# Loading and storing the first four rows of a layer-scale kernel by halves over two DMA rings

## The chip, the cores and the metric

The kernel runs on one core of one Trainium2 chip. The metric is device time in microseconds (us), as the median of several runs. Before the change it is 119.79 us (6 runs, 119.58 to 119.87).

## The reference

```python
x, y: bf16 [1024, 16, 512]      gamma: bf16 [512]
def reference(x, y, gamma):
    return x + gamma * y
```

Flattened, x, y and the output have 16,384 rows of 512 values, 1 KB each. So 16.8 MB of x and as much of y are read, and 16.8 MB are written.

## The kernel before

Each of the 128 partitions of the on-chip memory holds 128 rows of y (`y_sb`); the result is formed in place and stored from there. x has a smaller buffer (`x_sb`), parts of which are used twice. In what follows a "row" is one of these 128 places per partition, 0 to 127.

The rows are cut into three blocks (`BLOCKS`, L7) of 4, 64 and 60 rows. `rows_of` (L65) maps a block to a contiguous stretch of memory, in which partition p has the p-th share. For the first block, rows 0 to 3, this is 512 KB of memory, and partition p has 4096 B at 4096 p.

All loads and stores are issued from two engines, each with its own DMA ring. Their order is written out by hand:

- `SP` (L12): y 0:4, y 4:68, x 4:68, y 68:128, x 68:120, x 120:128.
- `ACT` (L20): x 0:4, gamma, and the stores of rows 4:68, 0:4 and 68:128.

The function `ring` (L113) issues such a list. Some issues are moved to the very start of the program, ahead of its start barrier (`EARLY`, L22: two of SP's, one of ACT's; L197 to L203). Before the issue with the number in `AHEAD` (L24: SP's third, ACT's second), a ring waits until TensorE has seen the load named `HOLD` land, which is y 0:4 (L147 to L149). VectorE gets the same signal. TensorE then waits for gamma, spreads it over the partitions with one matmul (L152), and VectorE copies it to `gamma_sb` (L154). A second signal from TensorE, when x 68:120 has landed (`RELEASE`, L157 to L159), lets ACT's stores begin.

VectorE works in five pieces (`PIECES`, L9) of 8, 16, 44, 52 and 8 rows. The list `DVE` (L28) is its order: multiply pieces 0, 1, 2; add pieces 2, 0, 1; multiply 3, 4; add 3, 4. Multiplications are L180, additions L189. Each waits for the loads that its piece meets (`need`, L163). x 68:120 and x 120:128 go to places of `x_sb` that earlier rows of x had, so their issue waits for additions (`frees`, L102; L126). A store waits for the additions of its rows. The program ends when all stores have reported on `s_out` (L195).

Of the kernel before, what the change touches and what calls it, by code (L numbers as in the profile page):

```python
# [8 lines left out]
PIECES = [8, 16, 44, 52, 8]  # L9


SP = [  # L12
    ('y', 0, 4),
    ('y', 4, 68),
    ('x', 4, 68, 4),
    ('y', 68, 128),
    ('x', 68, 120, 24),
    ('x', 120, 128, 0),
]
ACT = [('x', 0, 4, 0), ('g',), ('s', 4, 68), ('s', 0, 4), ('s', 68, 128)]  # L20

EARLY = (2, 1)  # L22

HOLD, AHEAD = ('y', 0, 4), (2, 1)  # L24

RELEASE = ('x', 68, 120, 24)

# [4 lines left out]
def _take(sem, n, eng):  # L32


    return eng.wait_ge(sem, n).then_inc(sem, -n)  # L35


def kernel(
    tc: tile.TileContext,
    x: bass.AP,  # L40
    y: bass.AP,
    gamma: bass.AP,
    out: bass.AP,
):

    nc = tc.nc
    P = nc.NUM_PARTITIONS
    tc.close()  # L50
    tc.compile()  # L51

    xf = x.flatten_outer_dims()
    yf = y.flatten_outer_dims()
    of = out.flatten_outer_dims()
    N, D = xf.shape
    rows = N // P
    n = len(PIECES)
    assert sum(PIECES) == rows
    starts = [sum(PIECES[:c]) for c in range(n + 1)]  # L60
    dt = xf.dtype
    edges = [sum(BLOCKS[:c]) for c in range(len(BLOCKS) + 1)]
    assert edges[-1] == rows

    def rows_of(t, a, b):  # L65

        c = max(c for c in range(len(BLOCKS)) if edges[c] <= a)
        assert b <= edges[c + 1]
        block = t[P * edges[c] : P * edges[c + 1]].rearrange("(p n) d -> p n d", p=P)
        return block[:, a - edges[c] : b - edges[c], :]  # L70

    gamma_row = nc.alloc_sbuf_tensor("gamma_row", [1, D], dt).ap()
    ones_row = nc.alloc_sbuf_tensor("ones_row", [1, P], dt).ap()
    gamma_sb = nc.alloc_sbuf_tensor("gamma_sb", [P, D], dt).ap()
    y_sb = nc.alloc_sbuf_tensor("y_sb", [P, rows, D], dt).ap()
    x_loads = [w for w in ACT + SP if w[0] == "x"]
    y_loads = [w for w in SP + ACT if w[0] == "y"]
    stores = [w for w in SP + ACT if w[0] == "s"]
    for loads in (x_loads, y_loads, stores):
        assert sum(w[2] - w[1] for w in loads) == rows  # L80
    x_rows = max(w[3] + w[2] - w[1] for w in x_loads)
    x_sb = nc.alloc_sbuf_tensor("x_sb", [P, x_rows, D], dt).ap()
    gamma_ps = nc.alloc_psum_tensor("gamma_ps", [P, D], mybir.dt.float32).ap()

    sem = nc.alloc_semaphore
    s_gamma, s_ones, s_ps, s_dve = sem("s_gamma"), sem("s_ones"), sem("s_ps"), sem("s_dve")
    s_load = {w: sem("s_" + "_".join(map(str, w[:2]))) for w in x_loads + y_loads}
    s_held = {nc.sync: sem("s_held_sp"), nc.scalar: sem("s_held_act"), nc.vector: sem("s_held_dve")}
    s_add, s_go, s_rel, s_end, s_out = sem("s_add"), sem("s_go"), sem("s_rel"), sem("s_end"), sem("s_out")
    added = [a for kind, *a in DVE if kind == "a"]  # L90
    order = {a[0]: k for k, a in enumerate(added)}

    def meets(a, b, c, d):
        return a < d and c < b

    def pieces_of(a, b):
        return [c for c in range(n) if meets(starts[c], starts[c + 1], a, b)]

    def x_at(row):
        return next(w[3] + row - w[1] for w in x_loads if w[1] <= row < w[2])  # L100

    def frees(w):  # L102

        c = set()
        for v in x_loads[: x_loads.index(w)]:
            lo, hi = max(v[3], w[3]), min(v[3] + v[2] - v[1], w[3] + w[2] - w[1])
            if lo < hi:
                c |= set(pieces_of(v[1] + lo - v[3], v[1] + hi - v[3]))
        return sorted(c)

    early = []

    def ring(eng, what, n_early, n_ahead):  # L113

        known, went = 0, False
        for k, w in enumerate(what):
            kind = w[0]
            if k == n_ahead:
                _take(s_held[eng], 1, eng)
            need = frees(w) if kind == "x" else pieces_of(w[1], w[2]) + list(w[3:]) if kind == "s" else []  # L120
            need = max((order[c] + 1 for c in need), default=0)
            if kind == "s" and not went:
                _take(s_go, 1, eng)
                went = True
            if need > known:
                eng.wait_ge(s_add, need)  # L126
                known = need
            if kind == "g":
                i = eng.dma_start(out=gamma_row, in_=gamma.unsqueeze(0)).then_inc(s_gamma, 16)
            elif kind == "x":  # L130
                to = x_sb[:, w[3] : w[3] + w[2] - w[1], :]
                i = eng.dma_start(out=to, in_=rows_of(xf, w[1], w[2])).then_inc(s_load[w], 16)
            elif kind == "y":
                r = slice(w[1], w[2])
                i = eng.dma_start(out=y_sb[:, r, :], in_=rows_of(yf, w[1], w[2])).then_inc(s_load[w], 16)
            else:
                r = slice(w[1], w[2])
                i = eng.dma_start(out=rows_of(of, w[1], w[2]), in_=y_sb[:, r, :]).then_inc(s_out, 16)
            if k < n_early:
                early.append(i.ins)  # L140

    ring(nc.sync, SP, EARLY[0], AHEAD[0])
    ring(nc.scalar, ACT, EARLY[1], AHEAD[1])


    nc.vector.memset(ones_row, 1.0).then_inc(s_ones, 1)  # L146
    _take(s_load[HOLD], 16, nc.tensor)  # L147
    for s_one in s_held.values():
        nc.tensor.sem_inc(s_one, 1)  # L149
    _take(s_ones, 1, nc.tensor)  # L150
    _take(s_gamma, 16, nc.tensor)
    nc.tensor.matmul(gamma_ps, ones_row, gamma_row, start=True, stop=True).then_inc(s_ps, 1)  # L152
    _take(s_ps, 1, nc.vector)
    nc.vector.tensor_copy(out=gamma_sb, in_=gamma_ps).then_inc(s_dve, 1)  # L154
    _take(s_dve, 1, nc.vector)

    _take(s_load[RELEASE], 16, nc.tensor)  # L157
    nc.tensor.sem_inc(s_go, 1)
    nc.tensor.sem_inc(s_rel, 1)  # L159

    landed, open_mults = set(), 0

    def need(loads, c):  # L163
        for w in loads:
            if w not in landed and meets(starts[c], starts[c + 1], w[1], w[2]):
                if w == RELEASE:
                    _take(s_rel, 1, nc.vector)
                elif w == HOLD:
                    _take(s_held[nc.vector], 1, nc.vector)
                else:  # L170
                    _take(s_load[w], 16, nc.vector)
                landed.add(w)

    for kind, *args in DVE:
        c = args[0]
        yt = y_sb[:, starts[c] : starts[c + 1], :]
        if kind == "m":
            need(y_loads, c)
            g = gamma_sb[:, None, :].to_broadcast([P, PIECES[c], D])
            nc.vector.tensor_tensor(out=yt, in0=yt, in1=g, op=MULT).then_inc(s_dve, 1)  # L180
            open_mults += 1
        else:
            need(x_loads, c)
            if open_mults:
                _take(s_dve, open_mults, nc.vector)
                open_mults = 0
            at = x_at(starts[c])
            xt = x_sb[:, at : at + PIECES[c], :]
            nc.vector.tensor_tensor(out=yt, in0=xt, in1=yt, op=ADD).then_inc(s_add, 1)  # L189


    nc.scalar.sem_inc(s_end, 1)
    _take(s_end, 1, nc.sync)
    _take(s_add, n, nc.sync)
    _take(s_out, 16 * len(stores), nc.sync)  # L195

    main = nc.main_func.blocks[0].instructions  # L197
    names = {i.name for i in early}
    for b in nc.main_func.blocks[1:]:
        for i in [i for i in b.instructions if i.name in names]:  # L200
            b.instructions.remove(i)
    for k, i in enumerate(early):
        main.insert(1 + k, i)  # L203
# [30 lines left out]
```

## Time and profile before

| | |
|---|---|
| Median of 6 runs | 119.79 us (119.58 to 119.87) |
| The profiled execution's own time | 119.92 us |
| Its span, first to last instruction | 118.6 us |
| Moved by DMA | 50.33 MB, 424 GB/s on the mean |
| VectorE busy | 70.1 us (59%) |
| Queue q1 (SP's ring) | 864 packets, 33.03 MB |
| Queue q10 (ACT's ring) | 578 packets, 17.30 MB |

The profile is one execution, seen instruction by instruction. The busy line gives each engine's share of the span. The line of digits named DMA cuts the span into 40 equal slices and gives the mean busy share of the core's 16 DMA engines in tenths. The queue lines give packets, megabytes and the share of 16 engines' time that their packets took. In a table of windows, the columns are the window, its length, the busy time of PE, PEld, DVE (VectorE) and POOL, the granted clock, the DMA share and GB/s; the bytes of a packet are counted in the window where it starts. In a timeline a line has start, duration, engine and line of the code; SPq and ACTq are the sequencers that issue DMAs, and their durations are those of the issue, not of the transfer. The list of DMA issues ends in the time from issue to landing.

### The profile page before, as it was taken

The numbers are of one execution on the slowest core, as the hardware profiler recorded it, in microseconds if no ns is written. First come the engines' busy times: TensorE is split into PE (matmuls) and PEld (weight loads), VectorE is DVE, ScalarE is ACT, GpSimd is POOL, SyncE is SP. The second block draws the span as 40 slices with busy tenths as digits, with TensorE's granted clock in tenths as the row PEclk, the third lists the DMA queues.
The fourth block names the chain that finished last, engine by engine and source line by source line (L and its number), as shares of the span: only waits on it lengthen the run. The fifth ranks groups of instructions, "written<-read, shape, count | busy, mean of one in ns | idle before, by whom it ended". The sixth has DMA issues, their size and how long they took to land. (4 is left out here: it accounts for less than half of the span.)

```text
span 118.6 us, 91 instructions
## 1 busy us (share of the span) xinstructions
PE 0.6 (0%) x1; PEld 0.1 (0%) x1; DVE 70.1 (59%) x12; POOL 0.2 (0%) x4
## 2 busy tenths in 40 slices
PE   0000100000000000000000000000000000000000
PEld 0000000000000000000000000000000000000000
DVE  0000200089999969999999999999999900000000
POOL 0000000000000000000000000000000000000000
DMA  6999888998899879977969797798899889799787
GB/s 202 506 398 663 354 354 354 641 420 354 354 553 508 354 332 518 477 332 332 663 287 557 305 557 305 337 658 354 354 508 553 354 354 508 332 580 414 332 352 311
DMA packets 1442, 50.33 MB, mean 424 GB/s; under 512 B 161, under 2 KB 162, under 8 KB 546
## 3 DMA queue, kind: packets, MB, share of 16 engines
q1 hardware_dynamic: 864, 33.03, 65.0%
q10 hardware_dynamic: 578, 17.30, 33.8%
HBM read 33.56 MB, written 16.78 MB: 424 GB/s over the span
## 5 line engine op out<-in xcount | busy, mean ns | idle before, releaser
L180 DVE TENSOR_TENSOR y_sb<-y_sb,gamma_sb 128x4096 bf16<-128x4096 bf16 (+3 forms) x5 | 34.6, 6979 | 11.1 <-DVEq L35 11.1
L189 DVE TENSOR_TENSOR y_sb<-x_sb,y_sb 128x4096 bf16<-128x4096 bf16 (+3 forms) x5 | 34.7, 6981 | 1.2 <-DVEq L35 1.0
L154 DVE CAST gamma_sb<-gamma_ps 128x512 bf16<-128x512 f32 x1 | 0.7, 692 | 10.4 <-DVEq L35 10.4
L146 DVE MEMSET ones_row<- 1x128 bf16 x1 | 0.2, 165 | 2.0 <-PEq L51 2.0
L152 PE MATMUL gamma_ps<-gamma_row,ones_row 1*128 1x512 bf16 x1 | 0.6, 578 | 11.8 <-PEq L35 11.8
L152 PEld LDWEIGHTS gamma_ps<-gamma_row,ones_row 1*128 1x128 bf16 x1 | 0.1, 100 | 11.8 <-issue 11.8
L218 POOL MEMSET const-bfloat16-1.0<- 128x1 bf16 x1 | 0.1, 102 | 0.0
L218 POOL MEMSET const-uint8-127<- 128x1 uint8 x1 | 0.1, 102 | 0.0
L218 POOL MEMSET const-float32-1.0<- 128x1 f32 x1 | 0.1, 99 | 0.0
L218 POOL MEMSET const-float32-0.0<- 128x1 f32 x1 | 0.1, 98 | 0.2 <-issue 0.2
## 6 DMA issues: line engine op xcount, KB each, us to landing
y_sb<-in_y_dram SPq DMA_DIRECT2D x1, 7680.0 KB, 57.3
out_dram<-y_sb ACTq DMA_DIRECT2D x1, 7680.0 KB, 23.8
x_sb<-in_x_dram SPq DMA_DIRECT2D x1, 6656.0 KB, 21.7
x_sb<-in_x_dram SPq DMA_DIRECT2D x1, 1024.0 KB, 22.0
y_sb<-in_y_dram SPq DMA_DIRECT2D x1, 512.0 KB, 3.7
x_sb<-in_x_dram ACTq DMA_DIRECT2D x1, 512.0 KB, 4.7
out_dram<-y_sb ACTq DMA_DIRECT2D x1, 512.0 KB, 22.3
y_sb<-in_y_dram SPq DMA_DIRECT2D x1, 23.7
```

The source lines that it names most:

```text
L146: nc.vector.memset(ones_row, 1.0).then_inc(s_ones, 1)
L152: nc.tensor.matmul(gamma_ps, ones_row, gamma_row, start=True, stop=True).then_inc(s_ps, 1)
L154: nc.vector.tensor_copy(out=gamma_sb, in_=gamma_ps).then_inc(s_dve, 1)
L180: nc.vector.tensor_tensor(out=yt, in0=yt, in1=g, op=MULT).then_inc(s_dve, 1)
L189: nc.vector.tensor_tensor(out=yt, in0=xt, in1=yt, op=ADD).then_inc(s_add, 1)
L218: nc = _bacc.Bacc("TRN2", target_bir_lowering=False, num_devices=1)
```

## The change

The loads of rows 0:4 of y and of x, and the store of these rows, become two DMAs each. Half 0 has the even partitions, half 1 the odd ones. Of the block's 512 KB of memory, half 0 has the first 256 KB and half 1 the second, so that each half is a stretch without gaps; partition 2k + h has the k-th 4096 B of half h. x, y and the output are cut alike. SP issues half 0 of y and of x ahead of y 4:68, ACT half 1 of y and of x ahead of gamma. ACT issues both halves of the store, one after the other, in the place of the one before. All the loads by halves and y 4:68 are issued early; the hold is now on both halves of y, which share one semaphore that TensorE waits on for 32.

```diff
 SP = [
-    ('y', 0, 4),
+    ('y', 0, 4, 'half', 0),
+    ('x', 0, 4, 0, 'half', 0),
     ('y', 4, 68),
     ('x', 4, 68, 4),
     ('y', 68, 128),
     ('x', 68, 120, 24),
     ('x', 120, 128, 0),
 ]
-ACT = [('x', 0, 4, 0), ('g',), ('s', 4, 68), ('s', 0, 4), ('s', 68, 128)]
-
-EARLY = (2, 1)
-
-HOLD, AHEAD = ('y', 0, 4), (2, 1)
+ACT = [
+    ('y', 0, 4, 'half', 1),
+    ('x', 0, 4, 0, 'half', 1),
+    ('g',),
+    ('s', 4, 68),
+    ('s', 0, 4, 'half', 0),
+    ('s', 0, 4, 'half', 1),
+    ('s', 68, 128),
+]
+
+EARLY = (3, 2)
+
+HOLD, AHEAD = [('y', 0, 4, 'half', h) for h in range(2)], (3, 2)
...
-        block = t[P * edges[c] : P * edges[c + 1]].rearrange("(p n) d -> p n d", p=P)
-        return block[:, a - edges[c] : b - edges[c], :]
+        part = t[P * edges[c] : P * edges[c + 1]]
+        if w[-2] == "half":
+            half = P // 2 * (edges[c + 1] - edges[c])
+            part = part[half * w[-1] : half * (w[-1] + 1)].rearrange("(p n) d -> p n d", p=P // 2)
+        else:
+            part = part.rearrange("(p n) d -> p n d", p=P)
+        return part[:, a - edges[c] : b - edges[c], :]
+
+    def at(sb, w, first):
+
+        parts = slice(w[-1], P, 2) if w[-2] == "half" else slice(0, P)
+        return sb[parts, first : first + w[2] - w[1], :]
...
-    s_load = {w: sem("s_" + "_".join(map(str, w[:2]))) for w in x_loads + y_loads}
+    s_load = {w: sem("s_" + "_".join(map(str, w[:2] + w[4:]))) for w in x_loads + y_loads if w not in HOLD}
+    s_hold = sem("s_hold")
+    s_load |= {w: s_hold for w in HOLD}
...
-    _take(s_load[HOLD], 16, nc.tensor)
+    _take(s_hold, 16 * len(HOLD), nc.tensor)
...
-                elif w == HOLD:
-                    _take(s_held[nc.vector], 1, nc.vector)
+                elif w in HOLD:
+                    if w == HOLD[0]:
+                        _take(s_held[nc.vector], 1, nc.vector)
```

## The prediction

> **What bounds the kernel now.** I read the page first: busy time, the 40 slices and the queues.
>
> ```profile
> span 118.6 us, 91 instructions
> PE 0.6 (0%) x1; PEld 0.1 (0%) x1; DVE 70.1 (59%) x12; POOL 0.2 (0%) x4
> DMA  6999888998899879977969797798899889799787
> ...
> DMA packets 1442, 50.33 MB, mean 424 GB/s; under 512 B 161, under 2 KB 162, under 8 KB 546
> ...
> q1 hardware_dynamic: 864, 33.03, 65.0%
> q10 hardware_dynamic: 578, 17.30, 33.8%
> ```
>
> No compute engine is near full: VectorE has 59%. The two DMA queues take 65.0 + 33.8 = 98.8% of the time of 16 DMA engines. Only the first slice (6) shows a real gap. So the time is a head before the first packet, 50.33 MB through 16 engines, and a tail. The chain of waits agrees in its own way: it holds only 10.6% issue and 3.2% VectorE of the span, because what happens inside DMA queues isn't in it.
>
> Next I read the DMA packet records of the trace (queue, start, duration, size). A 65,536 B packet takes 2418 ns, 27.1 GB/s for one engine; a 4096 B packet takes 159 ns, 25.8 GB/s; a completion record takes 9 ns and costs about 15 ns with the step to it. An engine starts its next packet as the last one ends, from about 1.0 to 1.4 us to 117.9 to 118.2 us. That is the proof that each nanosecond added to an engine's packets is added to the end. Reckoned per engine: busy 117.16 us, which with a mean start of 1.16 us makes 118.3 us.
>
> The head is the place of the change, so I cut it into stretches of 0.5 us (the last two columns are the DMA share and GB/s):
>
> ```profile
> 1.00:1.50 0.50, 0.00 (x0) 0.00 (x0) 0.00 (x0) 0.00 (x0) 1.00 1.06 156
> 1.50:2.00 0.50, 0.00 (x0) 0.00 (x0) 0.01 (x1) 0.00 (x0) 1.00 0.90 303
> 2.00:2.50 0.50, 0.00 (x0) 0.00 (x0) 0.16 (x1) 0.00 (x0) 1.00 1.04 393
> 2.50:3.00 0.50, 0.00 (x0) 0.00 (x0) 0.00 (x0) 0.00 (x0) 1.00 0.90 360
> 3.00:3.50 0.50, 0.00 (x0) 0.00 (x0) 0.00 (x0) 0.00 (x0) 1.00 1.04 418
> ```
>
> Bytes are booked where a packet starts, so only stretches of small packets read well. Sixteen engines with 4096 B in 159 ns make 412 GB/s. Against that the five rows lose 0.31 + 0.13 + 0.02 + 0.06 + 0 = about 0.5 us. More than 0.5 us can't be won in the head without an earlier first packet. In the records the first packet of an engine takes 501 ns on the mean (269 to 838), 0.34 us over 159 ns: most of that half microsecond. ACT's ring shows its first packet only at 2.57 us, after six or seven packets of SP's on each engine, although ACT issued at 0.13 us.
>
> The timeline gives the issues:
>
> ```profile
> 0.00 0.85 SPq L135 DMA_DIRECT2D y_sb<-in_y_dram  x2
> 0.13 0.38 ACTq L132 DMA_DIRECT2D x_sb<-in_x_dram  x1
> ...
> 1.99 0.17 DVE L146 MEMSET ones_row<- 1x128 bf16 x1 [1.99 <-PEq L51]
> 4.01 0.33 SPq L132 DMA_DIRECT2D x_sb<-in_x_dram  x1
> 4.21 0.50 ACTq L129 DMA_DIRECT2D gamma_row<-in_gamma_dram  x1
> ```
>
> and the issue list their landings:
>
> ```profile
> y_sb<-in_y_dram SPq DMA_DIRECT2D x1, 512.0 KB, 3.7
> x_sb<-in_x_dram ACTq DMA_DIRECT2D x1, 512.0 KB, 4.7
> ```
>
> [...]the 128 store packets of 4096 B at 98.5 to 100.1 us all took 159 ns. [...]Nothing in this trace is a half.
>
> **The change part by part.** All against the profiled execution's 119.92 us (span 118.6 us and 1.3 us around it), which is 0.13 us over the median of 119.79.
>
> *More DMAs.* Loads of y and x and the store become two each: 3 more completion records on every engine, 3 x 15 ns = 0.045 us, all on the path. Bytes and 4096 B packets stay: 24 an engine, as before.
>
> *Issue time.* SP has three early issues for two, ACT two for one. The step from SP's first issue to its second is 0.42 us. y 4:68 is then issued at 0.84 for 0.42 us; with 1.0 us from issue to first packet (SP's first: 0.00 to 1.006) its descriptors are there at 1.9 us and are needed at 3.98 us, when its first packet ran. Nothing, with 2 us of cover; 0.42 us if that were gone. The start barrier behind the issues (SP joins it at 0.90 us) moves by 0.42 us, and the memset with it, to 2.4 us; TensorE's wait for y ends at 3.7 us, so nothing. ACT's extra store issue (0.46 us at 78.6 us) lies before a wait until 94.7 us: nothing; 0.46 us without that.
>
> *The hold.* TensorE waits for both halves, 32 counts. Behind it are SP's x 4:68 and y 68:128 and ACT's gamma. y lies first in both rings now, so it lands between 3.0 and 3.7 us. x 4:68 has y 4:68 ahead of it in its ring until 23.7 us: 19 us of cover. gamma at 11.7 us is needed with y at 24.2 us: 12 us. Nothing either way. VectorE isn't what is late: the last store, issued at 94.74 us, waits in its ring until 99.8 us.
>
> *The start.* Two rings have descriptors for each engine at once, and each issue covers 64 partitions. Between 0 [...]and the 0.5 us above. Engines' first packets start over 0.37 us (1.006 to 1.379); half of that spread, on the mean 0.1 us, is what I take.
>
> *Ports.* Trace of before has no transfer with a partition step of 2, so I bound it. [...]packets would take 318 ns. Low end 0[...]. High end: all 24 packets, 24 x 0.159 = 3.8 us. [...]
>
> Sum: 0.045 - 0.1 + 1.7 = +1.65 us. 119.92 + 1.65 - 0.13 = 121.4 us.
>
> **The rivals.**
> Ports in conflict (forecast), 0.42: 121.0 to 123.3 us. [...]Against: no row shows sharing.
> No conflict, and the rings take turns as now, 0.30: +0.045 and 0 to -0.2, so 119.6 to 120.0 us. For it: ACT's packets came only after SP's first six or seven, so the second ring may again wait and the halves run one after the other; then the change doesn't do what it says.
> Faster start, the other side, 0.20: both rings feed each engine from 1.0 us and the cold first packets overlap. It recovers most of the 0.5 us, price -0.4 + 0.045, so 119.4 us (119.25 to 119.55). It decides where less than 0.3 us goes to ports. Against it: an engine's packets follow one another[...].
> A small loss, 0.08: conflict in the store alone or a late y 4:68, 0.3 to 1.2 us, 120.1 to 121.0.
>
> **How the numbers follow.** A measurement can tell about 0.2% (0.24 us) from no change, so faster is below 119.55 and slower above 120.03. Faster 0.20, same 0.29 (most of the second case), slower 0.51. The range goes from 119.4 to 123.0: it leaves out half of the fast case and the far end of the conflict. The likeliest case alone has 121.0 to 123.3.
>
> **What would show it.** Right: 4096 B packets of 250 to 318 ns in the records at 1.5 to 5 us and again in the store near 100 us; stretches of some 250 GB/s there; y 4:68 landing after 25 us (24.2 now). Packets of 159 ns in both places would refute the ports. A first ACT packet near 1.1 us and stretches of 400 GB/s by 1.5 us would show the faster start. SP's third issue should stand near 0.84 us and the memset near 2.4 us. The prediction is wrong if [...]something outside the rings moves, such as y 4:68's first packet starting after a gap.

## The result and the profile after

| | before | changed |
|---|---|---|
| Median | 119.76 us (119.58 to 120.05, 35 runs) | 121.26 us (120.02 to 122.06, 17 runs) |
| Ratio | 1 | 1.0099, 95% interval 1.0078 to 1.0119 |
| The profiled execution | 119.92 us, span 118.6 us | 121.66 us, span 120.3 us |

The ratio is below 121.26 / 119.76 because it compares means, not medians, and leaves out the two highest runs as slow ones. By it the changed kernel is slower by about 1.2 us. Its times are no longer within 0.4% of each other: six of the 17 runs lie at 120.0 to 120.5 us, eleven at 120.8 to 122.1 us. The profiled execution is one of the long ones, 1.74 us over the one of before.

The page of the changed kernel:

```profile
span 120.3 us, 95 instructions
DMA  5989888988898889789779798898898889798790
...
DMA packets 1490, 50.33 MB, mean 418 GB/s; under 512 B 209, under 2 KB 210, under 8 KB 594
...
q1 hardware_dynamic: 880, 33.03, 64.1%
q10 hardware_dynamic: 610, 17.30, 33.5%
```

The bytes are the same. There are 48 more packets, all under 512 B: the 3 x 16 completion records that were counted in the prediction. Nothing else was added, and yet 418 GB/s stands for 424. The engines must therefore be idle somewhere or work slower. The timeline shows the issues of the head:

```profile
0.00 0.55 SPq L157 DMA_DIRECT2D y_sb<-in_y_dram  x1
0.12 0.55 ACTq L157 DMA_DIRECT2D y_sb<-in_y_dram  x1
...
0.60 0.58 SPq L155 DMA_DIRECT2D x_sb<-in_x_dram  x1
0.71 0.74 ACTq L155 DMA_DIRECT2D x_sb<-in_x_dram  x1
1.23 0.59 SPq L157 DMA_DIRECT2D y_sb<-in_y_dram  x1
2.96 0.17 DVE L167 MEMSET ones_row<- 1x128 bf16 x1 [2.96 <-PEq L62]
```

SP's issue of half of y takes 0.55 us; the issue of all of y took 0.37 us before. y 4:68 is issued at 1.23 us, not 0.42, and takes 0.59 us for the same transfer. The windows of the head (last column GB/s):

```profile
1.00:1.50 0.50, 0.00 (x0) 0.00 (x0) 0.00 (x0) 0.00 (x0) 1.00 0.82 82
1.50:2.00 0.50, 0.00 (x0) 0.00 (x0) 0.00 (x0) 0.00 (x0) 1.00 0.51 49
2.00:2.50 0.50, 0.00 (x0) 0.00 (x0) 0.00 (x0) 0.00 (x0) 1.00 0.93 377
2.50:3.00 0.50, 0.00 (x0) 0.00 (x0) 0.04 (x1) 0.00 (x0) 1.00 1.03 418
3.00:3.50 0.50, 0.00 (x0) 0.00 (x0) 0.12 (x1) 0.00 (x0) 1.00 1.07 434
...
5.00:5.50 0.50, 0.00 (x0) 0.00 (x0) 0.00 (x0) 0.00 (x0) 1.00 0.37 131
```

Two things are to be seen. The first two rows have 82 and 49 GB/s where before had 156 and 303: the engines start later. In the last row, 131 GB/s over 0.5 us is 65,536 B: a single 64 KB packet starts there, alone. It is the first packet of y 4:68 on one engine. The DMA packet records, from which the following table is drawn up, say it exactly:

```
first packets of y 4:68, one per engine, start us
before:  3.98 4.03 4.04 4.07 4.11 4.12 4.14 4.14 4.16 4.16 4.17 4.18 4.20 4.20 4.38 4.49
changed: 4.36 4.36 4.37 4.38 4.41 4.42 4.43 4.45 4.49 4.56 4.58 4.58 4.60 4.62 4.66 5.40
         the last one took 2940 ns, the usual time is 2418 ns
packets of 4096 B      median ns   over 250 ns      first packets start us
before, loads             159          29           1.006 to 1.379
changed, loads            159          16           1.336 to 1.643
changed, store            159           0
```

The records carry no engine number. But all small packets had ended by 4.7 us, and fifteen 64 KB packets were running, so one engine had nothing to do from about 4.6 to 5.4 us, and then a slow first packet. It never makes this up: y 4:68 lands on fifteen engines by 24.42 us and on the last at 25.62; x 68:120 by 77.79 and 78.88; the last 61,440 B store packets end at 118.97 to 119.11 us and 119.93. The store signal needs all of x 68:120, so the stores began to be issued at 79.23 us for 77.78. For the first of them the other engines had to wait: between 79 and 81 us the sixteen stood idle for 7.2 us in all, some 0.45 us each, where before none was idle. They still ended about 0.8 us ahead of the late one.

So in this execution about 0.35 us comes from a later start of all engines, and most of the rest from one late engine. The experiments ask what makes each. Times below are medians; where two kernels are compared, I multiply the difference of their ratios to the kernel before by 119.76 us. The diffs show only the lines that differ.

### The profile page after: what moved, and what is told of

Same layout as the page of the kernel before. It is cut to its first block, busy times and chain, and to the rows that moved or that the text cites. A ratio compares the mean times of both kernels' runs of the same rounds, so it can differ in the third digit from the quotient of the medians.

```text
span 120.3 us, 95 instructions
## 1 busy us (share of the span) xinstructions
PE 0.6 (0%) x1; PEld 0.1 (0%) x1; DVE 70.1 (58%) x12; POOL 0.2 (0%) x4
## 3 DMA queue, kind: packets, MB, share of 16 engines
q1 hardware_dynamic: 880, 33.03, 64.1%
q10 hardware_dynamic: 610, 17.30, 33.5%
```

## The experiments

### Loads or store

```diff
 e1 (against the changed kernel)
-    ('s', 0, 4, 'half', 0),
-    ('s', 0, 4, 'half', 1),
+    ('s', 0, 4),
```


> Loads by halves, the store of rows 0:4 whole again (its four rows come out in another order than the reference's, since the store no longer undoes the halves' order). Theory A (the loss is at the start: later first packets on all engines, +0.35 us, and in most runs one DMA engine that gets its descriptors of y 4:68 late, +1.2 us): as the changed kernel, 120.0 to 122.0 us, median 121.2, with a gap of about 0.7 us on one engine before its first 64 KB packet. Rival B (the store by halves costs as well): 0.3 us or more below the changed kernel.

Measured 121.65 us (120.45 to 121.91, 6 runs), ratio 1.0134 (1.0096 to 1.0173). Two groups again: 120.45 and 120.51, then 121.54 and more. In its profile two engines began y 4:68 at 6.06 and 6.22 us, the others by 4.79.

```diff
 e2 (against the changed kernel)
 SP:  -('y', 0, 4, 'half', 0), ('x', 0, 4, 0, 'half', 0)    +('y', 0, 4)
 ACT: -('y', 0, 4, 'half', 1), ('x', 0, 4, 0, 'half', 1)    +('x', 0, 4, 0)
-EARLY = (3, 2)
+EARLY = (2, 1)
 and HOLD, AHEAD = [('y', 0, 4)], (2, 1)
```


> Loads whole as before, only the store by halves (its rows come out in another order). Theory A: as before, 119.7 to 119.9 us, the small store's packets at 159 ns. Rival B (store): slower than before by 0.3 us or more. The ports that the prediction went by: +0.6 to +0.9 us, packets near 318 ns in the store.

Measured 119.73 us (119.59 to 119.97, 13 runs), ratio 1.0001 (0.9993 to 1.0009). All 128 packets of the small store took 159 ns. The store by halves costs nothing that can be measured. What the prediction calls ports is the assumption that two engines delay each other's packets; no run had shown that, and none of these packets came near 318 ns. With e1 beside it, the whole loss is in the loads.

### Do packets of halves get slow at all?

```diff
 e3 (against the changed kernel)
-        parts = slice(w[-1], P, 2) if w[-2] == "half" else slice(0, P)
+        parts = slice(P // 2 * w[-1], P // 2 * (w[-1] + 1)) if w[-2] == "half" else slice(0, P)
```


> Halves are partitions 0 to 63 and 64 to 127 in place of even and odd ones; memory addresses unchanged. If the number of DMAs and of partitions in each makes the loss (theory A in its simple form): 121.2 us as the changed kernel. If the partition step of 2 is what makes the issue long (0.55 us for 0.37): first packets at 1.0 us again and 119.8 to 120.2 us. If port sharing exists here at all, it shows as 4096 B packets well over 159 ns.

Measured 123.90 us (123.26 to 124.66, 6 runs), ratio 1.0345 (1.0315 to 1.0376). Issues stayed at 0.56 and 0.58 us and first packets at 1.36 us, so the step of 2 is not what makes an issue long. And the small packets now are slow, 281 ns in the median for the loads and 223 ns for the store (up to 753). Three windows of the loads:

```profile
2.00:3.00 1.00, 0.00 (x0) 0.00 (x0) 0.04 (x1) 0.00 (x0) 1.00 1.08 311
3.00:4.00 1.00, 0.00 (x0) 0.00 (x0) 0.13 (x1) 0.00 (x0) 1.00 1.04 229
4.00:5.00 1.00, 0.00 (x0) 0.00 (x0) 0.00 (x0) 0.00 (x0) 1.00 1.06 234
```

The engines are shown as fully busy at 229 GB/s, a little over half of 412. This is the kind of cost that I had forecast for even and odd partitions. What makes the packets slow here wasn't shown. The even/odd cut, with 159 ns in the median, shows none of it.

### Which part of the loads

```diff
 e4 (against the changed kernel)
 SP:  -('y', 0, 4, 'half', 0), ('x', 0, 4, 0, 'half', 0), ('y', 4, 68)
      +('y', 0, 4, 'half', 0), ('y', 4, 68)
 ACT: -('y', 0, 4, 'half', 1), ('x', 0, 4, 0, 'half', 1), ('g',)
      +('y', 0, 4, 'half', 1), ('x', 0, 4, 0), ('g',)
 EARLY = (2, 2), AHEAD = (2, 2)
```


> Only y 0:4 is loaded by halves (SP and ACT), x 0:4 whole on ACT's ring after its half of y, so y 4:68 is SP's second DMA again (rows 0:4 of the output pair x and y of different places). If the late descriptors come of y 4:68 being third and late on SP (theory A1): 120.0 to 120.2 us, the later start alone, no engine with a gap. If they come of halves issued on both sequencers at once (A2): 121 us or more in most runs, as the changed kernel.

Measured 122.50 us (122.47 to 122.65, 4 runs), ratio 1.0233 (1.022 to 1.0247). Neither theory had foreseen that. There was no late engine: y 4:68 began at 2.92 to 3.17 us on all sixteen. The loss is elsewhere, as the timeline shows, with two lines of before first:

```profile
24.30 18.43 DVE L180 TENSOR_TENSOR y_sb<-y_sb,gamma_sb 128x4096 bf16<-128x4096 bf16 x3 [11.06 <-DVEq L35]
...
55.69 2.53 SPq L132 DMA_DIRECT2D x_sb<-in_x_dram  x2
```

and those of e4:

```profile
4.03 0.49 ACTq L152 DMA_DIRECT2D gamma_row<-in_gamma_dram  x1
29.04 0.10 PEld L172 LDWEIGHTS gamma_ps<-gamma_row,ones_row 1*128 1x128 bf16 x1 [29.04 <-issue]
...
30.86 18.43 DVE L201 TENSOR_TENSOR y_sb<-y_sb,gamma_sb 128x4096 bf16<-128x4096 bf16 x3 [0.37 <-DVEq L45]
...
61.36 2.53 SPq L154 DMA_DIRECT2D x_sb<-in_x_dram  x2
```

y 4:68 now began before x 0:4 was through. The engines took packets of the two rings in turn (from 5 to 22.5 us, 16 packets of 4 KB of x for 16 of 64 KB of y in every 2.5 us), so x landed at 24.4 us and gamma behind it at 28.94 us (11.7 before). The first multiplication started at 30.86 us for 24.30, x 68:120 was issued at 61.36 us for 55.69 and landed at 79.99 us for 77.43. A next kernel tests this reading:

```diff
 e10 (against e4; x by halves, the store by halves)
 ACT: -('y', 0, 4, 'half', 1), ('x', 0, 4, 0), ('g',)
      +('y', 0, 4, 'half', 1), ('g',), ('x', 0, 4, 0, 'half', 0), ('x', 0, 4, 0, 'half', 1)
```


> SP issues half 0 of y and y 4:68 early; ACT half 1 of y and gamma early, then both halves of x after the hold, behind gamma; store by halves. Only one half lies ahead of y 4:68. Theory: the 122.5 us of the kernel with y alone by halves came of gamma, which had eight packets of x per engine ahead of it in ACT's ring while 64 KB packets ran in SP's (it landed at 28.9 us for 11.7); with gamma first, 120.0 to 120.5 us, and no late engine, since y 4:68 isn't behind two halves. Rival: in that kernel late descriptors were at work as well; then 121 us or more, with engines that begin y 4:68 late or idle before it.

Measured 120.31 us (120.07 to 120.53, 5 runs), ratio 1.0043 (1.0028 to 1.0057). gamma landed at 8.26 us, and 2.2 of the 2.8 us that e4 had lost are gone. So most of e4's loss was its own, an order in ACT's ring. Of late engines e4 and e10 say only that one half directly ahead of y 4:68, with nothing before it in SP's ring, left none idle.

### One sequencer or two, partitions or rows

```diff
 e5 (against the changed kernel)
 SP:  +both halves of y, both halves of x, then ('y', 4, 68)
 ACT: -the half of y and the half of x
 EARLY = (5, 0), AHEAD = (5, 0)
```


> All four half loads issued by SP, ACT issues nothing early: the same five DMAs in one ring. Theory A2 (both sequencers issuing at once share something that makes descriptors: issues are longer and one engine's come late): issues back near 0.37 us, first packets near 1.0 us, no late engine; 119.8 to 120.1 us. Rival A3 (a DMA of 64 partitions is slow to issue by itself): issues stay at 0.55 us, first packets at 1.34 us, y 4:68 issued after 2.2 us; 120.1 us or more.

Measured 121.51 us (120.98 to 122.53, 6 runs), ratio 1.0151 (1.0118 to 1.0185). With ACT silent SP's issues were 0.55, 0.58, 0.59, 0.60 and 0.59 us. Theory A2, the two sequencers in each other's way, is out. The late engines stay: y 4:68, issued at 2.50 us, began at 4.57 to 4.68 us on eight engines and at 5.30 to 5.60 us on the other eight.

```diff
 e6 (against the changed kernel; store whole)
 SP:  -('y', 0, 4, 'half', 0), ('x', 0, 4, 0, 'half', 0)    +('y', 0, 2), ('x', 0, 2, 0)
 ACT: -('y', 0, 4, 'half', 1), ('x', 0, 4, 0, 'half', 1)    +('y', 2, 4), ('x', 2, 4, 2)
```


> The same rings and the same number of early DMAs, but the cut is by rows (0:2 and 2:4) and every DMA has 128 partitions with 2048 B each; the store is whole. A2 (number of DMAs and two sequencers at once): as the changed kernel, above 121 us in most runs, with a late engine. A3 (64 partitions): issues of 0.37 to 0.43 us, first packets at 1.0 us, no late engine, 119.8 us and 0.1 to 0.2 us on top for twice the packets of half the size.

Measured 120.22 us (120.06 to 120.37, 8 runs), ratio 1.0032 (1.002 to 1.0044). There are five early DMAs as in the changed kernel, but of 128 partitions. SP's issues in the timeline:

```profile
0.00 0.36 SPq L156 DMA_DIRECT2D y_sb<-in_y_dram  x1
...
0.41 0.43 SPq L154 DMA_DIRECT2D x_sb<-in_x_dram  x1
...
0.89 0.43 SPq L156 DMA_DIRECT2D y_sb<-in_y_dram  x1
```

First packets of y 4:68 came at 4.21 to 4.55 us on all engines, and the times are one group. A3 stands, though 120.22 us is 0.2 to 0.3 us over what it gave: the shape of the DMAs counted here, not their number or the rings. A DMA of 64 partitions also has 64 packets here and one of 128 has 128; no run tells these two apart.

```diff
 e9 (against the changed kernel)
 SP:  +('y', 0, 4, 'half', 0), ('y', 0, 4, 'half', 1), ('y', 4, 68)
 ACT: +('x', 0, 4, 0, 'half', 0), ('x', 0, 4, 0, 'half', 1), ('g',)
```


> Both halves of y on SP and both of x on ACT, as the whole loads lay before. As many early DMAs on each ring as in the changed kernel. A2 and A3 both: as the changed kernel, 120.0 to 122 us with most above 121. If sharing each tensor between the rings is what costs: 119.8 to 120.1 us.

Measured 121.47 us (120.32 to 122.30, 6 runs), ratio 1.012 (1.0085 to 1.0155), with one late engine (4.97 us, first packet 3307 ns). So whether SP's second half is one of x or of y made no difference that shows (121.47 us for 121.26).

### When y 4:68 is issued

```diff
 e8 (against the changed kernel)
-EARLY = (3, 2)
+EARLY = (2, 2)
```


> The changed kernel with y 4:68 issued after the start barrier and not before, so SP has two early issues. If the late descriptors come of five issues in a row before the barrier (pile-up): no engine with a gap beyond that of all others, 120.0 to 120.6 us in all runs. If they come of the halves themselves: a late engine still, 121 us and more in most runs.

Measured 120.32 us (120.24 to 120.55, 6 runs), ratio 1.0045 (1.0031 to 1.0059). In its timeline y 4:68 is issued later, at 2.77 us for 1.23, in 0.34 us for 0.59:

```profile
0.60 0.58 SPq L155 DMA_DIRECT2D x_sb<-in_x_dram  x1
...
2.77 0.34 SPq L157 DMA_DIRECT2D y_sb<-in_y_dram  x1
```

It began on all engines by 4.69 us. The upper group of times is gone, and what stays is like the changed kernel's lower group. A later issue made the kernel faster: that rules out that y 4:68 was simply issued too late.

```diff
 e11 (against the changed kernel; store whole)
 SP:  -('y', 0, 4, 'half', 0), ('x', 0, 4, 0, 'half', 0), ('y', 4, 68)
      +('y', 0, 4), ('x', 0, 4, 0, 'half', 0), ('y', 4, 68)
 ACT: -('y', 0, 4, 'half', 1), ('x', 0, 4, 0, 'half', 1)
      +('x', 0, 4, 0, 'half', 1)
 EARLY = (3, 1), HOLD = [('y', 0, 4)], AHEAD = (3, 1)
 e13 (against e11)
-EARLY = (3, 1)
+EARLY = (2, 1)
```


> y 0:4 whole on SP as before; only x 0:4 by halves, half 0 on SP between y 0:4 and y 4:68, half 1 on ACT; store whole (rows 0:4 pair x and y of different places). Theory on the start: SP's first issue takes 0.37 us again and first packets begin at 1.0 us, so the 0.3 us of the later start are gone. Theory on the late engine: it takes 64-partition DMAs directly ahead of y 4:68 on SP; if one is enough, 121 us and a gap on an engine in most runs; if two are needed (backlog), 119.8 to 120.0 us and no gap.

> As the kernel with y 0:4 whole and x 0:4 by halves on both rings (121.0 us), but y 4:68 issued after the start barrier. If its loss is y 4:68 issued directly behind a half: 119.8 to 120.1 us, with first packets at 1.0 us and no engine idle ahead of y 4:68. If the half's own descriptors are the late ones: 120.5 us or more.

e11: 121.04 us (120.88 to 121.27, 4 runs), ratio 1.0116 (1.01 to 1.0132). e13: 119.89 us (119.79 to 120.16, 21 runs), ratio 1.0016 (1.001 to 1.0023). In both kernels rows 0:4 pair x and y of different places. The timelines, e11 first:

```profile
0.00 0.37 SPq L155 DMA_DIRECT2D y_sb<-in_y_dram  x1
...
0.42 0.53 SPq L153 DMA_DIRECT2D x_sb<-in_x_dram  x1
1.00 0.58 SPq L155 DMA_DIRECT2D y_sb<-in_y_dram  x1
```

```profile
0.00 0.37 SPq L155 DMA_DIRECT2D y_sb<-in_y_dram  x1
...
0.42 0.53 SPq L153 DMA_DIRECT2D x_sb<-in_x_dram  x1
2.25 0.33 SPq L155 DMA_DIRECT2D y_sb<-in_y_dram  x1
```

In both, y 0:4 whole is issued in 0.37 us and first packets stand at 1.0 us again: the later start goes with a half as the first DMA. They differ only in when y 4:68 is issued. Issued at 1.00 us, right behind a half, y 4:68 has first packets that start as late as 5.25 us, nine of the sixteen take 3.3 to 3.9 us, and the kernel is at 121.04 us. Issued at 2.25 us, it has all of them started by 4.25 us, they take 2.75 us at most, and the kernel is at 119.89 us. That is (1.0116 - 1.0016) x 119.76 = 1.2 us for one number in the code. In e11's profile most of it is in the long packets: on the mean of the sixteen engines they take 0.63 us longer than in e13 and start 0.31 us later, and the two profiled executions differ by 0.95 us.

```diff
 e12 (against e11)
 SP:  -('x', 0, 4, 0, 'half', 0)
 ACT: +('x', 0, 4, 0, 'half', 0), ('x', 0, 4, 0, 'half', 1)
 EARLY = (2, 2), AHEAD = (2, 2)
```


> SP's ring exactly as before (y 0:4 whole, y 4:68); x 0:4 by halves, both on ACT; store whole (rows 0:4 pair x and y of different places). If the lateness stays in the ring in which a half lies ahead (SP's): as before, 119.7 to 120.0 us, y 4:68's first packets of 2.4 to 2.7 us. If a half on either ring slows the supply of descriptors for both: 120.5 us or more, with first 64 KB packets over 3 us or an engine with a gap.

Measured 120.03 us (119.78 to 120.39, 13 runs), ratio 1.0021 (1.0012 to 1.0031), between the two expectations. y 4:68 began at 3.23 to 3.62 us on all engines, its first packets took up to 3.0 us. Halves in ACT's ring alone did little, (1.0021 - 1) x 119.76 = 0.25 us; the large loss was seen only with one ahead of y 4:68 in SP's.

## Why the prediction was right in size and wrong in cause

The forecast was 121.4 us, and 121.26 us was measured, within the range and on the side that had 0.51. The number held by luck: the term that made nearly all of it came to nothing, and terms that were put at nothing or below made up for it.

- **Ports (+1.7 us): failed.** The step was "packets would take 318 ns", twice the 159 ns of before. That, and the 1.7 us taken between 0 and 3.8 us, were my estimates; no trace showed two engines delaying each other. In the median the packets took 159 ns in loads and store, in e1, e2, e8 and e13 as well, and the store by halves cost nothing (e2). The assumption led to the wrong answer; which partitions each engine takes isn't in a trace. Of the signs named for it, only the landing of y 4:68 after 25 us came (25.62), and one late engine made that. Slow packets do exist where the halves are lower and upper, 281 ns in the loads and 223 ns in the store in the median (e3), from a cause that wasn't shown.
- **Issue time ("nothing, with 2 us of cover"): failed, and here most of the loss was.** I took the 0.42 us between SP's first two issues of before for the new ones too. A load of 64 partitions took SP 0.53 to 0.60 us, and y 4:68 right behind one 0.57 to 0.59 us; it was issued at 1.23 us, not 0.84. ACT's second half of the store took 1.40 us to issue for the 0.46 forecast, but ahead of a wait, so at no cost. Worse, issue plus 1.0 us isn't when every engine can begin: y 4:68 began on one engine 4.2 us after its issue. By e8 against the changed kernel, the early issue of y 4:68 costs (1.0099 - 1.0045) x 119.76 = 0.6 us on the mean, over runs with and without a late engine.
- **The start (-0.1 us): wrong sign.** The premise, two rings that feed each engine from the start, failed: ACT's ring, issued at 0.12 us, shows its first packet only at 2.48 us, after 58 packets of SP's ring, whose half of y has 64; so y's halves ran nearly one after the other, as the second rival had feared. And SP's first packets came later, at 1.336 us for 1.006. In all eight profiles with a half as SP's first DMA the first packet is at 1.34 to 1.62 us, in the six with a whole one at 1.00 to 1.12 us. e8 and e13 differ in having y 0:4 by halves or whole, with the store's form besides, which is worth nothing: (1.0045 - 1.0016) x 119.76 = 0.35 us. In their profiles the first packets of y 4:68 start on the mean at 4.41 and 4.03 us, which fits a later start by about as much.
- **Completion records (+0.045 us): consistent.** 48 more are there. What is left in e13, (1.0016 - 1) x 119.76 = 0.2 us, holds one more record per engine and the two halves of x; it wasn't split further.
- **The hold: right.** y was there at 3.74 us, gamma at 12.04 us for a use at 25.8 us. But e4 shows how thin the cover of gamma is in another order of ACT's ring: it landed at 28.94 us, and the first multiplication began at 30.86 us for 24.30.

So 1.2 us is about 0.6 (y 4:68 right behind a half) + 0.35 (later first packets) + 0.2, each uncertain by 0.1 to 0.3 us by the intervals. Of the rivals, the "small loss" named the cause, "a late y 4:68", and had 0.08; its range, 120.1 to 121.0 us, ends below the median of 121.26. One reading of the prediction was off by little: the first packets of before start on the mean at 1.145 us, not 1.16; nothing rests on it. The rival of no conflict gave 119.6 to 120.0 us, because it had the issue for free. The faster start was wrong: the first packets moved the other way. The sign to look for was named well, 159 ns "in both places would refute the ports", and so was "y 4:68's first packet starting after a gap".

**Still open.** Why a DMA of 64 partitions took longer to issue than one of 128 (0.53 to 0.60 us for 0.37 on SP), why the first packet of all came later with one in front (1.34 to 1.62 us for 1.00 to 1.12), and why a DMA right behind it started late on one, two or eight engines (the changed kernel, e1, e5). That some executions have no late engine is inferred from the lower group of times; no execution of that group was profiled for the changed kernel. The large loss took both a half close ahead in the same ring and no pause (e6, e8, e12, e13 lack one of them); these two aren't enough, since one half as the only DMA ahead left no engine idle (e4, e10). The late issue also lies behind the start barrier, and no run has the pause without the barrier. That it is descriptors which come late is my reading: the trace shows late and long first packets, not what holds them back.

No kernel here beat the one before. e2, which loads everything whole, was level with it; of those with a load by halves e13 came nearest, 0.2 us behind.

## What to carry to other kernels

Here the DMA engines were busy for 97.6% of the span (64.1 + 33.5), and the stall of one of them from about 4.6 to 5.4 us showed up at the end (its last packet ended at 119.93 us, those of the others by 119.11): look at when each engine starts its first large packet, not at the mean. Price an issue by the shape of the very transfer that is issued, not by another row (0.42 us was taken, 0.53 to 0.60 us measured), and look for spread-out run times: a cost that comes only in some executions, here by their times in eleven of 17, need not show in the one that is profiled. Cutting a transfer that already keeps all engines busy had at most 0.5 us to win here and lost 1.2.

## What the runs showed of the hardware that was not expected

- On SP, the issue of a 64-partition load took 0.53 to 0.60 us, that of y 0:4 with 128 partitions 0.37 us; the same y 4:68 took 0.43 us behind a DMA of 128 partitions, 0.57 to 0.59 us behind one of 64, and 0.33 to 0.34 us after a pause. On ACT, a half behind another half took 0.60 to 0.77 us.
- ACT's ring began later than SP's: with its first issue at 0.12 to 0.13 us, its first packet came at 2.05 to 2.64 us in all thirteen profiles in which it issued early, SP's at 1.00 to 1.62 us.
- Packets of 4096 B took 159 ns in halves by even and odd partitions, as in whole transfers; in lower and upper halves the loads took 281 ns and the store 223 ns in the median.
- The engines took packets of two rings in turn, 4 KB against 64 KB, 16 of each in every 2.5 us: eight packets of 4 KB per engine beside 64 KB packets made the 1 KB of gamma land at 28.9 us for 11.7 (e4).
